# Fused attention and feed-forward on one core: product 2 of seven accumulates onto a copied product 1, more seven-product units, one explicit order for all work

## The chip, the cores and the metric

The kernel runs on one core of a Trainium2 chip. The metric is the device time of one execution in microseconds (us). A core has TensorE (matmuls, "PE", with weight loads as "PEld"), VectorE ("DVE"), ScalarE ("ACT"), GpSimd ("POOL") and SyncE ("SP"); POOL, SP and ACT also issue DMAs. Matmuls write PSUM, which has eight banks of 512 f32 a partition.

## What is computed

Squared-relu attention without a softmax, and on its output a feed-forward block with a gated unit:

```python
scores = (1/sqrt(64)) * q @ k.T          # batch 8, 12 heads, sequence 448, head 64
attn = maximum(scores, 0)**2 / 448
x = (attn @ v) -> (3584, 768)            # heads side by side
g, val = x @ w_gate, x @ w_val           # (768, 1536) each
out = (gelu(g) * val) @ w_out            # (1536, 768)
```

Inputs and output are f32; the kernel computes in bf16 with f32 sums in PSUM.

## The kernel before, in words

**The array.** All large matmuls use a quarter of the array (64 rows by 64 columns, `mm`, line 364, recorded at line 365). The upper and lower row halves are two streams, PE0 and PE1 in the code; each step of a stream is two matmuls, one for each column half.

**The stages.** For each batch, `add_scores` (line 677) makes 21 score units (a relu on ACT, L714, then a square on DVE, L728). `add_values` (line 761) makes six pairs of heads of x, transposed as xT, which are copied from PSUM (L792). `add_gate_value` (line 1023) makes one block of 128 columns of gate or of value with six steps of 448 columns; the gate ends in a gelu (L1044), the value in a multiply (L1049) that writes uT. The last stage, `add_product` (line 1160), makes the output in 14 groups (a to n), each with seven products instead of eight (384 columns wide, copied or added at L1225 and L1223).

**Seven-product units.** Part of gate and value is done in the same manner: `add_pair` (line 911) takes two blocks of gate and of value of a batch as a two by two product, split into halves of the depth and of the tokens, with seven products of six steps of 224 columns. `NPB` (line 317) says how many such units each batch has: 0, 1, 2, 3, 4, 4, 6, 6, in all 26. They need sums of weights (`add_pair_sums`, line 845, four DVE adds) and sums of tokens (`add_token_sums`, line 887). Products 1, 6, 5 and 3 go one after another through one PSUM bank (X), 7 and 4 through a second (Y), 2 has a third (Z). Products 1, 6 and 7 are copied to SBUF by ACT (L962, the tile `part`); 2, 4 and 5 are added to these copies by DVE (L966); then ACT takes the gelu (L970) and DVE multiplies (L975).

**The order.** Nothing is ordered by hand at the level of instructions. Each step becomes an `Op` with a cost, an engine and what it depends on; `run_plan` (line 109) then walks through time and writes the program engine by engine. A later piece of TensorE work is a `Unit`; `next_unit` takes from the next 40 (`AHEAD`) of a list the first that can start at once, together with the bank that came free first. The list is sorted by a place, `at`. For gate, value, units and products the place comes from the string `LINE`: a digit is the next gate or value block of that batch, `3B6` is product 6 of unit B of batch 3, `d7` is product 7 of output group d. Scores and values have places worked out from those of the blocks, moved by the numbers in `SHIFT`. Batch 0's attention follows a list of its own, `START`.

**Banks.** Two banks at first, later one pair, hold scores; six (`FB + 2`) serve all the rest. A Z bank is taken when product 2 starts.

**Loads.** POOL issues the loads of q, k and v and of all weights in one order; from batch 2 on they wait for relus of earlier thirds of a batch (a third is four heads). From batch 2 on q and k are regrouped by DVE (L475) and transposed by DMAs that SP issues (L480), between the stores of the output (L1241).

## Time and profile before

| what | us |
|---|---|
| three timed runs, median | 403.09 |
| three timed runs, lowest and highest | 400.13, 404.37 |
| span of the profiled execution | 394.9 |

The profiled execution has its span, from the first to the last instruction, and no time of its own beside it; the timed runs hold also what lies around the span.

The profile shows one execution. Each group of instructions has a line number, an engine, what it writes and reads, its shape and a count; then its busy time, the mean of one in ns, and the idle time of its engine just before it with what ended that. "PE" is busy from the start to a modelled end of a matmul, and matmuls overlap, so how fast the array runs is read from the distance between starts.

### The profile page before, as it was taken

Reading aid. Unit: us, or ns where it says so; the run is one execution under the profiler, and the core shown is the slowest. Engines: PE = TensorE matmul, PEld = TensorE weight load, DVE = VectorE, ACT = ScalarE, POOL = GpSimd, SP = SyncE. Lnnn points to the kernel's source line nnn. Section 1 sums busy time; section 2 is a strip of 40 time slices with the busy share of each in tenths; the row PEclk is TensorE's granted clock in tenths of the full one; section 3 lists DMA queues with packets and bytes.
Section 4 is the critical chain, followed back from the end, with each engine's and each line's share of the span. In section 5 each row is a group of like instructions: output and inputs, shape, how many; then the busy total and the mean of one; then the engine's idle time right before and its main releaser. Section 6 shows DMA issues by size and latency. Waiting matters only on the chain.

```text
span 394.9 us, 22904 instructions
## 1 busy us (share of the span) xinstructions
PE 386.3 (98%) x10570; PEld 358.4 (91%) x10573; DVE 309.6 (78%) x522; ACT 258.7 (66%) x401; POOL 97.2 (25%) x156
## 2 busy tenths in 40 slices
PE   7999999999999999999999999999999999999995
PEld 3458889999999999999999999989999999999994
DVE  3885779968797499999797779758988999866772
ACT  5866872357677767787786478765787886535541
POOL 7656523322233323232332123310211000000000
PEclk9999999999999999999999999999999999999999
DMA  8999999988999969887999598880763501121134
GB/s 110 186 199 199 197 209 185 112 103 83 161 148 175 152 85 143 93 132 121 113 148 108 124 122 111 139 83 11 103 105 56 125 6 43 45 45 45 43 85 120
DMA packets 85567, 45.12 MB, mean 114 GB/s; under 512 B 46048, under 2 KB 82400, under 8 KB 85472
## 3 DMA queue, kind: packets, MB, share of 16 engines
q0 software_dynamic: 46944, 24.39, 49.9%
q1 hardware_dynamic: 37888, 18.49, 26.4%
q8 instruction: 82, 1.34, 1.4%
q10 hardware_dynamic: 640, 0.79, 0.6%
q14 instruction: 13, 0.11, 0.1%
HBM read 48.76 MB, written 11.01 MB: 151 GB/s over the span
## 4 chain that ended last, share of the span: by engine, by line
PE 93%; DVE 2%; DMA 2%; POOL 1%; issue 1%; ACT 0%; ACTq 0%; POOLq 0%
PE ff L365 85%; PE sp L365 7%; DMA qk<-in_k_dram 2%; DVE attnT L728 1%; PE sp L646 1%; POOL qk L424 1%; DVE xT L792 0%; PE ff L646 0%; ACTq L1241 0%; ACT osb L1225 0%; ACT rl L714 0%; PE ff L567 0%; DVE osb L1223 0%; DVE qkT L650 0%; POOL ident masks.py:199 0%
## 5 line engine op out<-in xcount | busy, mean ns | idle before, releaser
L714 ACT ACTIVATE rl<-sp 128x896 bf16<-128x896 f32 x168 | 152.1, 919 | 50.4 <-PE sp L365 45.1
L365 PE MATMUL ff<-xT,wg 64*64 64x224 bf16 (+1 forms) x2304 | 183.7, 299 | 0.6 <-issue 0.6
L365 PEld LDWEIGHTS <-wv 64*64 64x64 bf16 x2304 | 127.7, 107 | 4.4
L365 PEld LDWEIGHTS <-wg 64*64 64x64 bf16 x2304 | 123.3, 107 | 5.0 <-issue 0.5
L365 PE MATMUL ff<-xT,wv 64*64 64x448 bf16 x1056 | 120.8, 349 | 0.0
L728 DVE TENSOR_TENSOR attnT<-rl 128x1792 bf16<-128x1792 bf16 (+1 forms) x98 | 92.2, 952 | 6.6 <-ACT rl L714 6.2
L365 PEld LDWEIGHTS <-ws 64*64 64x64 bf16 x1872 | 92.3, 107 | 1.4 <-issue 1.0
L365 PEld LDWEIGHTS <-s 64*64 64x64 bf16 x1344 | 81.6, 107 | 1.8
L365 PE MATMUL ff<-attnT,v 64*64 64x448 bf16 (+1 forms) x768 | 79.7, 326 | 0.7 <-DVE attnT L728 0.6
L365 PE MATMUL ff<-ts,wv 64*64 64x224 bf16 x1248 | 78.7, 256 | 0.0
L365 PE MATMUL ff<-ts,ws 64*64 64x224 bf16 x1248 | 77.6, 256 | 0.0
L365 PE MATMUL sp<-qkT 64*64 64x448 bf16 (+1 forms) x768 | 74.6, 328 | 0.7 <-issue 0.3
L365 PE MATMUL ff<-wo,s 64*64 64x384 bf16 x672 | 63.4, 323 | 0.0
L966 DVE TENSOR_TENSOR part<-ff,part 128x448 f32<-128x448 f32 x78 | 47.5, 622 | 20.1 <-PE ff L365 16.4
L365 PEld LDWEIGHTS <-uT 64*64 64x64 bf16 x1008 | 62.5, 107 | 0.7
L365 PE MATMUL ff<-wt,s 64*64 64x384 bf16 x672 | 61.4, 322 | 0.0
L365 PE MATMUL ff<-wo,uT 64*64 64x384 bf16 x672 | 60.7, 322 | 0.0
L962 ACT COPY part<-ff 128x448 f32<-128x448 f32 x78 | 41.3, 534 | 12.4 <-PE ff L365 11.2
L443 POOL DMA_DIRECT2D v<-in_v_dram x48 | 29.6, 620 | 80.3 <-ACT rl L714 44.3
L365 PEld LDWEIGHTS <-v 64*64 64x64 bf16 x768 | 44.7, 107 | 4.1 <-issue 1.7
L424 POOL DMA_DIRECT2D qk<-in_q_dram x43 | 27.6, 642 | 80.0 <-ACT rl L714 59.5
L1049 DVE TENSOR_TENSOR uT<-gel,ff 128x448 bf16<-128x448 bf16 x44 | 27.3, 620 | 22.4 <-PE ff L365 11.0
(51 smaller groups left out, 423.9 us busy)
## 6 DMA issues: line engine op xcount, KB each, us to landing
out_dram<-osb SPq DMA_DIRECT2D x48, 192.0 KB, 3.3
v<-in_v_dram POOLq DMA_DIRECT2D x48, 128.0 KB, 4.1
wg<-in_moe_w_gate_dram POOLq DMA_DIRECT2D x6, 384.0 KB, 10.4
wv<-in_moe_w_val_dram POOLq DMA_DIRECT2D x6, 384.0 KB, 11.0
wo<-in_moe_w_out_dram POOLq DMA_DIRECT2D x4, 576.0 KB, 14.9
qk<-in_q_dram POOLq DMA_DIRECT2D x18, 128.0 KB, 3.5
qk<-in_k_dram POOLq DMA_DIRECT2D x18, 128.0 KB, 4.3
qk<-in_q_dram POOLq DMA_DIRECT2D x18, 96.0 KB, 3.8
```

Source lines behind the costliest of these rows:

```text
L365: ins = nc.tensor.matmul(o, lhsT, rhs, start=start, stop=stop, skip_group_check=onto, tile_position=(P * row, P * col))
L424: return nc.gpsimd.dma_start(qk16[b, m][HALF[i], r0:r0 + h1 - h0, cols], src[b, h0:h1].rearrange("h (p c) d -> p h (c d)", c=SC)[:, :, cols])
L443: return nc.gpsimd.dma_start(v16[b, m][HALF[i], h0 % 4:h0 % 4 + h1 - h0, :, :], v[b, h0:h1].rearrange("h (p c) d -> p h c d", c=SC)[:, :, ...
L646: blocks.add(nc.tensor.transpose(t[HALF[j], c, :], src[:, 2 * r + j, c, :], ident[:, :], tile_position=(0, P * j)))
L714: relu.ins = nc.scalar.activation(duo["rl"][:, u % 2, :, :], box[0][:, :, 0:S], AF.Relu).ins
L728: nc.vector.tensor_tensor(a[:, part], duo["rl"][:, part], duo["rl"][:, part], op=ALU.mult)
L962: rd.ins = nc.scalar.copy(st["t", name][:, :], box[0][:, 0:S]).ins
L966: rd.ins = nc.vector.tensor_tensor(t[:, :], box[0][:, 0:S], t[:, :], op=ALU.add).ins
L1049: u_op[b, fc].ins = nc.vector.tensor_tensor(uT[b][:, fc, :], gel.pop((b, fc))[:, :], box[0][:, 0:S], op=ALU.mult).ins
```

## The change

- **Product 2.** At product 1 the unit now takes two banks, X and Z (`more` in `Unit` and `next_unit`). ACT copies product 1 from X into Z (`emit_seed`), and product 2 accumulates onto it there, so it waits for that copy. The gelu reads Z. The DVE add of product 2 and the SBUF copy of product 1 are gone.
- **Covers.** `full` notes whether a bank's last work had written all its columns. Where it had not (output products, 384 columns), two matmuls of zeros over the remaining columns come first.
- **Banks in the planner.** Work that opens a bank, and isn't the first of its kind in the list, is held back unless `SPARE` (2) banks remain beside those it needs.
- **xT copies.** From batch 1 on such a copy is offered to DVE and to ACT and goes to the first that is free. Before, the second offer stood at the end of a list of which the planner looks at the first 48; now it looks at all.
- **Units.** `NPB` becomes 0, 2, 4, 4, 4, 4, 6, 6, in all 30. (The words that came with the change say 28; `NPB` and `LINE` both hold 30.)
- **The order.** `LINE` now also places scores (`s`), values (`v`), transposes (`t`) and the weight sums (`w3` for pair 3); `SHIFT` and the places worked out from it are gone.

```diff
@@ -10,19 +10,23 @@
...
 LINE = """
-0 0 0 0 0 0 0 0 0 0 0 0 0 0 0 0 0 0 0 0 0 0 0 0 1 1A1 1 2 1A6 2 2 1 1A7 1A2 1A5 2 a1 2 a2 2A1 1A4 1
-1 1 1A3 1 2 1 2A2 a6 1 2A7 a7 2 1 a5 1 1 2A6 2 2 1 1 1 1 a3 1 1 a4 1 1 b1 b7 c1 b2 b6 2A4 2 c6 b4 b5
...
-7F4 7D6 7D5 7D4 7D3 l2 7F5 7A4 7C5 7C3 7E3 7A3 l5 l4 7F3 m1 n1 m7 k3 l3 m2 m6 n6 m5 n7 n4 m3 n5 n2
-m4 n3
+s s s s s s s t s s 0 0 0 s 0 0 0 s s s s t 0 0 s s s s s v 0 v s 0 0 0 0 0 0 v v s s s s 0 0 0 0 0
+v v 0 1 1 a7 1 s 1 w2 0 s s s s s s 1 1A1 1 1 1A2 a1 s 1B1 a6 1 1 w3 w1 s s s w0 1A6 s 1A7 a4 1B7
...
+c1 b7 c7 c6 s b1 b6 b4 b5 2A1 c4 s s s s v 2 2 2 b2 b3 2A6 2A7 2 2B1 2B6 c5 2B7 v v 2B2 2B4 2 2A2
...
+k6 k4 7C1 7C6 7F7 7F5 7F4 7F3 7D4 7B1 7C2 7B2 7C7 7C5 7E1 k5 7B6 7B7 7E7 l5 7B5 7B4 7B3 7D5 7D3 7C4
+7A3 7E6 7E5 7C3 7E2 7E4 m1 m7 7E3 m2 n1 n2 l2 l3 k3 m6 n6 n7 m5 n4 m3 n5 n3 m4
...
@@ -30,9 +34,6 @@
 t00 s0 s1 t01 s2 s3 s4 s5 t10 s6 s7 v0 s8 t11 v1 s9 s10 s11 t20 s12 s13 v2 s14 t21 s15 v3 s16 s17
 s18 s19 v4 s20
 """
-
-
-SHIFT = "-183 -79.5 40.75 1.75 -343.75 -112 43.75 -179.5 27.25 -513.5 -447.25 0.25"
 class Op:
@@ -96,17 +97,20 @@
 class Unit:
-    def __init__(self, at, los, his, box=None, closer=None, prev=None):
+    def __init__(self, at, los, his, box=None, closer=None, prev=None, more=None, full=True):
         self.at, self.los, self.his, self.box, self.closer, self.prev = at, los, his, box, closer, prev
+        self.more, self.full = more, full
         self.begun = False
         self.short = False
 AHEAD = 40
 BANK = 0.3
-
-
-def run_plan(queues, pools, units, banks, arrivals, together, fill, blocks, span):
+COVER = 0.06
+SPARE = 2
+
+
+def run_plan(queues, pools, units, banks, full, arrivals, together, fill, blocks, span):
@@ -157,10 +161,16 @@
     def next_unit(short):
         best = None
+        first = True
+        rest = sum(c is None or c.end is not None for c in banks.values())
         now = max(free["PE0"], floor)
         for u in units[:AHEAD]:
             if u.prev is not None and not u.prev.begun or short and not u.short:
                 continue
+            if u.box is not None:
+                if not first and rest < SPARE + 1 + (u.more is not None):
+                    continue
+                first = False
             t = ready(u.los[0])
             if t is None:
                 continue
@@ -184,11 +194,20 @@
                 if k is None:
                     continue
                 t = max(t, end + BANK)
+            k2 = None
+            if u.more is not None:
+                for n, c in banks.items():
+                    x = 0.0 if c is None else c.end
+                    if n != k and n in full and x is not None and (k2 is None or x < end):
+                        k2, end = n, x
+                if k2 is None:
+                    continue
+                t = max(t, end + BANK)
             if short and t > now:
                 continue
             t = max(t, now)
             if best is None or t < best[0]:
-                best = (t, u, k)
+                best = (t, u, k, k2)
                 if t <= now:
                     break
         return best
@@ -215,7 +234,7 @@
                     best = (key, "PE0", found)
         for e, ops in pools.items():
             mine = None
-            for op in ops[:48]:
+            for op in ops:
                 r = ready(op)
                 if r is not None:
                     t = max(r, free[e], floor if e in together else 0.0)
@@ -231,12 +250,20 @@
         forced = False
         (t, _, _), e, op = best
         if isinstance(op, tuple):
-            _, u, k = op
+            _, u, k, k2 = op
             u.begun = True
             units.remove(u)
             if k is not None:
                 u.box["k"] = k
                 banks[k] = u.closer()
+                full[k] = u.full
+            if k2 is not None:
+                u.more[0]["k"] = k2
+                banks[k2] = u.more[1]()
+                if not full[k2]:
+                    u.more[0]["cover"] = True
+                    u.los[0].cost += COVER
+                full[k2] = True
             queues["PE0"][at["PE0"]:at["PE0"]] = u.los
             pools["PE1"] += u.his
             op = u.los[0]
@@ -314,10 +341,11 @@
     EARLY = 2
     GATE_T, BLOCK = 1.2, 7.1
-    NPB = (0, 1, 2, 3, 4, 4, 6, 6)
+    NPB = (0, 2, 4, 4, 4, 4, 6, 6)
     ROOM = 4
     RING_V, RING_T, RING_H, RING_R, RING_A, RING_O = 3, 3, 2, 2, 4, 4
     SINGLE = "3"
+    RING_L = 2
     RING_M, RING_G = 5, 4
     out_scale = 1.0 / (D * S)
...
@@ -534,7 +562,7 @@
     def next_scores(at):
         n = len(units)
-        if at > WIDE and n % SB == 0 or wide:
+        if n >= WIDE and n % SB == 0 or wide:
             if not wide:
                 wide.append(0)
                 until.update({FB: at, FB + 1: at})
...
@@ -810,6 +838,8 @@
             x_op[b, pr] = Op("DVE", 0.575, emit_copy, [o_op[b, pr]], lag=0.2, prio=1,
                              other=("ACT", 0.5, emit_scaled) if b else None)
             DVE.append(x_op[b, pr])
+            if x_op[b, pr].other is not None:
+                ACT.append(x_op[b, pr])
         bank_read(box["k"], x_op[b, pr])
         if last:
             ops[1][0].after = ops[0][1]
@@ -916,11 +946,15 @@
             add_token_sums(b)
         st = pair_state.setdefault((b, unit), {})
         stage = stages[name]
-        if name in opens:
+        if name in "17":
             st["box", stage] = {}
             free = []
+        elif name == "2":
+            free = [st["read", "1"]]
         else:
             free = [st["read", stage]]
+        if name == "1":
+            st["box", "Z"] = {}
         box = st["box", stage]
         i = blocks[0] * 128 // WCH
         a = {"1": lambda: wg[i][:, KTOP, :], "2": lambda: wg[i][:, KEND, :], "3": lambda: ws[4, i],
@@ -937,6 +971,12 @@
         def emit(r, k):
             if 0 not in box:
                 box[0] = new_bank(box["k"], st["read", stages_last[stage]])
+            if (r, k, name) == (0, 0, "1"):
+                z = st["box", "Z"]
+                z[0] = new_bank(z["k"], st["read", "2"])
+                if "cover" in z:
+                    for j in range(2):
+                        mm(z[0][HALF[j], OGS:], warm[HALF[0], HALF[j]], warm[HALF[0], 0:512 - OGS], 0, j, False, False, True)
             if r == 1 and k == 0:
                 wait_lower(box)
             mov = ts[b, x][:, :, :] if isinstance(x, int) else xT[x[0]][:, x[1], x[2]]
@@ -945,7 +985,7 @@
             for j in range(2):
                 ins = mm(box[0][HALF[j], f * HS:(f + 1) * HS],
                          a()[HALF[r], c, o + P * j:o + P * (j + 1)], mov[HALF[r], c, :], r, j,
-                         name in opens and r == 0 and k == 0, r == 1 and c == K3 - 1, True)
+                         name in "17" and r == 0 and k == 0, r == 1 and c == K3 - 1, True)
             box[1] = ins
         ops = [[Op(f"PE{r}", HW, lambda r=r, k=k: emit(r, k),
@@ -956,6 +996,9 @@
             ts_used[b, x].append(last)
         else:
             reads_x.setdefault(x[0], []).append(last)
+
+        def emit_seed():
+            rd.ins = nc.scalar.copy(st["box", "Z"][0][:, 0:S], box[0][:, 0:S]).ins
         def emit_copy():
             st["t", name] = mpool.tile([128, S], f32, name="part", tag="part")
@@ -997,17 +1040,17 @@
                 u_op[to, f] = m
             return m
-        if name in "167":
+        if name == "1":
+            rd = Op("ACT", 0.5, emit_seed, [last], lag=0.2, prio=0)
+            ACT.append(rd)
+        elif name in "67":
             rd = Op("ACT", 0.5, emit_copy, [last], lag=0.2, prio=0)
             rd.takes = part_ring, lambda: st.get(("end", name))
             ACT.append(rd)
-        elif name in "245":
-            of = {"2": "1", "4": "6", "5": "7"}[name]
+        elif name in "45":
+            of = {"4": "6", "5": "7"}[name]
             rd = Op("DVE", 0.58, lambda: emit_add(of), [last, st["read", of]], lag=0.2, prio=0)
             DVE.append(rd)
-            if name == "2":
-                g = gelu(lambda: st["t", "1"][:, :], [rd], 0.2)
-                st["end", "1"] = g
             st["sum", name] = rd
         else:
             rd = gelu(lambda: box[0][:, 0:S], [last], 0.06)
@@ -1017,7 +1060,8 @@
             st["half"] = mult("2", "6", b0, c0, rd)
         if name == "3":
             mult("3", "7", b1, c1, st["sum", "5"], st["half"])
-        then(at, GS, *ops, box if name in opens else None, lambda: st["read", stages_last[stage]])
+        then(at, GS, *ops, box if name in "17" else None, lambda: st["read", stages_last[stage]],
+             (st["box", "Z"], lambda: st["read", "2"]) if name == "1" else None)
     def add_gate_value(at, b, fc, g):
...
@@ -1301,81 +1345,44 @@
...
+    flow = [[("g", b, fc, g) for fc in range(2 * NPB[b], FC) for g in range(2)] for b in range(B)]
+    flow_s = [(b, u) for b in range(1, B) for u in range(NU)]
+    flow_v = [(b, pr) for b in range(1, B) for pr in range(NPAIR)]
+    flow_t = [(1, m, (0, 1)) for m in range(1, NM)]
     work = []
-    flow = [[("g", b, fc, g) for fc in range(2 * NPB[b], FC) for g in range(2)] for b in range(B)]
-    line = []
...
+    for x in START.split():
+        at = placed0[x.rstrip("a")]
+        n = int(x.rstrip("a")[1:])
+        if x[0] == "t":
+            work.append((at, add_transposes, (0, n // 10, (n % 10,))))
+        else:
+            work.append((at, {"s": add_scores, "v": add_values}[x[0]], (0, n)))
+    work.append((PLACE5, add_values, (0, NPAIR - 1)))
+    work.append((PLACE5 + 0.05, add_transposes, (1, 0, (0, 1))))
+    for g in range(2):
+        work.append((0.0, add_gate_value, flow[0].pop(0)[1:]))
+    for n, x in enumerate(LINE.split()):
+        at = 1.0 + n
+        if x[0] == "w":
+            work.append((0.0, lambda at, i: add_pair_sums(i), (int(x[1]),)))
+        elif x == "s":
+            work.append((at, add_scores, flow_s.pop(0)))
+        elif x == "v":
+            work.append((at, add_values, flow_v.pop(0)))
+        elif x == "t":
+            work.append((at, add_transposes, flow_t.pop(0)))
+        elif len(x) == 1:
+            work.append((at, add_gate_value, flow[int(x)].pop(0)[1:]))
         elif len(x) == 3:
-            line.append(("7", int(x[0]), "ABCDEFGHIJKL".index(x[1]), x[2]))
+            work.append((at, add_pair, (int(x[0]), "ABCDEFGHIJKL".index(x[1]), x[2])))
         else:
-            line.append(("p", "abcdefghijklmn".index(x[0]), x[1]))
-    assert not any(flow)
-    at = 0.0
-    starts = [None] * B
-    placed = []
-    for item in line:
-        if item[0] == "g" and starts[item[1]] is None:
-            starts[item[1]] = at
-        if item[0] == "7" and starts[item[1]] is None:
-            starts[item[1]] = at
-        placed.append((at, item))
-        at += {"g": G, "7": G / 2, "p": R}[item[0]]
-    starts.append(at)
-    WIDE = 20.0
-    for at, item in placed:
-        if item[0] == "g":
-            work.append((at, 5, add_gate_value, item[1:]))
-        elif item[0] == "7":
-            work.append((at, 5, add_pair, item[1:]))
-        else:
-            _, gr, name = item
-            work.append((at, 5, add_product, (gr, name, gr == B * SC // 4 - 1)))
-    LEAD = 6.0
...
-    LO1 = 2.0
-    for b in range(B):
-        if b == 0:
-            lo, hi = -60.0, -12.0
-        elif b == 1:
-            lo, hi = LO1, starts[1] - LEAD
...
-        if b >= EARLY:
-            lo, hi = lo + float(SHIFT.split()[2 * (b - 2)]), hi + float(SHIFT.split()[2 * (b - 2) + 1])
-        if b >= EARLY:
-            lo = max(lo, passed)
-            hi = max(hi, lo + 1.0)
-        passed = hi
-        step = (hi - lo) / NU
...
-            work.append((x, 2, add_values, (b, pr)))
-        for u in range(NU):
-            work.append((placed0[f"s{u}"] if b == 0 else lo + u * step, 3, add_scores, (b, u)))
-    work.sort(key=lambda w: w[:2])
-    for i in reversed(range(max(NPB))):
-        behind = [n for n, w in enumerate(work) if w[2] is add_gate_value and w[3][0] == first_use(i) - 1][-1]
-        work.insert(behind + 1, (0.0, 5, lambda at, i: add_pair_sums(i), (i,)))
-
-
-    for at, _, fn, args in work:
+            gr = "abcdefghijklmn".index(x[0])
+            work.append((at, add_product, (gr, x[1], gr == B * SC // 4 - 1)))
+    assert not any(flow) and not flow_s and not flow_v and not flow_t
+    WIDE = 44
+
+
+    for at, fn, args in work:
         fn(at, *args)
@@ -1457,13 +1464,13 @@
     for made in (x_op, x_first):
         for (b, pr), op in made.items():
             op.deps += reads_x.get(b - 2, ())
-    for op in [*ACT, *DVE]:
-        if op.other is not None:
-            (DVE if op.engine == "ACT" else ACT).append(op)
-
     banks = {k: readers.get(k, [None])[-1] for k in range(FB + 2)}
+    full = {}
     run_plan({"PE0": PE0, "POOL": POOL}, {"PE1": PE1, "ACT": ACT, "DVE": DVE, "SP": SP, "IDLE": IDLE}, later,
-             banks, arrivals, ("PE0", "PE1"), fill, blocks, BLOCK)
+             banks, full, arrivals, ("PE0", "PE1"), fill, blocks, BLOCK)
+    if not rest:
+        for pool in loaded:
+            pool.__exit__(None, None, None)
 # ---- launch: one core; inputs and outputs as the reference has them ----
```

51 lines of the change are left out of this document (17 added, 34 removed).

## The prediction, on record before the change was run

> **What bounds the kernel now.** I read the page first (busy shares and the chain that ended last), then the busy time by stretches, then the groups of matmuls by shape, then what TensorE waited for.
>
> ```profile
> PE 386.3 (98%) x10570; PEld 358.4 (91%) x10573; DVE 309.6 (78%) x522; ACT 258.7 (66%) x401; POOL 97.2 (25%) x156
> ...
> PE 93%; DVE 2%; DMA 2%; POOL 1%; issue 1%; ACT 0%; ACTq 0%; POOLq 0%
> ```
>
> TensorE is busy nearly all the time and is 93% of the chain. A busy TensorE need not run at full rate, so the next question is how far apart its matmuls start. Three timelines give that, one for each width of the moving operand (first column: start in us).
>
> ```profile
> 78.48 0.38 PE L365 MATMUL ff<-xT,wv 64*64 64x448 bf16 x2
> ...
> 79.05 0.38 PE L365 MATMUL ff<-xT,wv 64*64 64x448 bf16 x2
> ```
>
> ```profile
> 264.44 0.26 PE L365 MATMUL ff<-ts,wv 64*64 64x224 bf16 x2
> ...
> 265.01 0.26 PE L365 MATMUL ff<-xT,ws 64*64 64x224 bf16 x2
> ```
>
> ```profile
> 387.49 0.32 PE L365 MATMUL ff<-wt,uT 64*64 64x384 bf16 x1
> ...
> 388.13 0.32 PE L365 MATMUL ff<-wt,uT 64*64 64x384 bf16 x1
> ```
>
> On one row half of the array two matmuls (its two column halves) start together. Three steps of 448 columns take 0.57 us, six of 224 take 0.57, four of 384 take 0.64: a step is 0.190, 0.095 and 0.160 us, and four matmuls (two row halves) share it. Now the groups by shape, with their counts:
>
> ```profile
> L365 PE MATMUL ff<-xT,wv 64*64 64x448 bf16 x1056 | 120.8, 349 | 0.0
> L365 PE MATMUL ff<-xT,wg 64*64 64x448 bf16 x1056 | 119.3, 349 | 0.0
> L365 PE MATMUL ff<-ts,wv 64*64 64x224 bf16 x1248 | 78.7, 256 | 0.0
> L365 PE MATMUL ff<-ts,ws 64*64 64x224 bf16 x1248 | 77.6, 256 | 0.0
> L365 PE MATMUL ff<-xT,wg 64*64 64x224 bf16 x1248 | 76.0, 256 | 0.6 <-issue 0.6
> L365 PE MATMUL ff<-attnT,v 64*64 64x448 bf16 x576 | 72.7, 349 | 0.7 <-DVE attnT L728 0.6
> L365 PE MATMUL sp<-qkT 64*64 64x448 bf16 x576 | 64.7, 351 | 0.4 <-ACT qkT L617 0.2
> L365 PE MATMUL ff<-wo,s 64*64 64x384 bf16 x672 | 63.4, 323 | 0.0
> L365 PE MATMUL ff<-wt,s 64*64 64x384 bf16 x672 | 61.4, 322 | 0.0
> L365 PE MATMUL ff<-wo,uT 64*64 64x384 bf16 x672 | 60.7, 322 | 0.0
> L365 PE MATMUL ff<-xT,ws 64*64 64x224 bf16 x624 | 39.6, 256 | 0.0
> L365 PE MATMUL ff<-wt,uT 64*64 64x384 bf16 x336 | 34.1, 323 | 0.0
> L365 PE MATMUL ff<-attnT,v 64*64 64x224 bf16 x192 | 26.6, 257 | 0.1
> L365 PE MATMUL sp<-qkT 64*64 64x224 bf16 x192 | 11.0, 257 | 0.3 <-issue 0.3
> ```
>
> 448 columns: 3264 matmuls, 816 steps of 0.190 = 155 us. 224 columns: 4752, 1188 steps of 0.095 = 113 us. 384 columns: 2352, 588 steps of 0.160 = 94 us. Together 362 of the 394.9 us of the span: the array streams at full rate for 92% of the time, and only 33 us are not that. Where these lie, by stretches (us, then busy time of PE, PEld, DVE, ACT, POOL):
>
> ```profile
> 0.00:26.00 26.00, 22.25 (x298) 11.48 (x305) 17.18 (x33) 19.70 (x24) 17.74 (x32) 1.00 1.16 160
> 26.00:57.00 31.00, 30.94 (x664) 25.36 (x658) 21.13 (x29) 20.67 (x28) 14.80 (x22) 1.00 1.37 201
> 57.00:250.00 193.00, 193.00 (x5166) 184.65 (x5162) 160.01 (x266) 131.24 (x200) 55.49 (x89) 1.00 0.94 128
> 250.00:270.00 20.00, 19.35 (x640) 18.63 (x634) 13.40 (x24) 13.48 (x24) 3.06 (x5) 1.00 0.72 92
> 270.00:385.00 115.00, 115.00 (x3718) 113.52 (x3713) 95.68 (x171) 72.42 (x125) 6.12 (x10) 1.00 0.32 61
> ```
>
> The first 26 us hold batch 0's attention, about 8 us of streaming (an eighth of the attention groups above: 288 steps of 0.190 and 96 of 0.095), so some 18 are lost there. From 57 to 385 there is nothing to win but work itself: the granted clock is 1.00, TensorE has no idle time but 0.65 us between 250 and 270 (the 0.6 "issue" of the 224-column xT,wg group above). DVE (160.0 of 193) and ACT (131.2) have room. So the change must pay in TensorE's steps, or in the small gaps.
>
> **The change, part by part.**
>
> *Units.* The words that came with the change say 28, but the new table of units per batch, (0, 2, 4, 4, 4, 4, 6, 6), and the units named in the new order both make 30, against 26; I go by these. A unit replaces two blocks of gate and value, 4 groups of 6 steps of 448 columns (24 x 0.190 = 4.56 us), by seven products of 6 steps of 224 (42 x 0.095 = 3.99). It saves 0.57 us; four more save **2.3 us**. With an error of 0.01 us on each of the two intervals the saving per unit could be 0.4 to 0.75, so 1.6 to 3.0.
>
> *Product 2 on a copied product 1.* Vector and scalar work by these rows:
>
> ```profile
> L966 DVE TENSOR_TENSOR part<-ff,part 128x448 f32<-128x448 f32 x78 | 47.5, 622 | 20.1 <-PE ff L365 16.4 <-ACT part L962 3.1
> ...
> L962 ACT COPY part<-ff 128x448 f32<-128x448 f32 x78 | 41.3, 534 | 12.4 <-PE ff L365 11.2 <-DVE uT L975 0.3
> ...
> L792 DVE TENSOR_SCALAR xT<-ff 128x448 bf16<-128x448 f32 x48 | 29.8, 622 | 7.1 <-PE ff L365 6.7
> ```
>
> DVE loses one add per unit (26 x 0.622 = 16.2 us). Each of the four added units brings it two adds, and its two multiplies stand for two of the same size that go: 4 x 2 x 0.622 = +5.0. DVE ends 11 us lower. ACT keeps its copy of product 1 (now into a PSUM bank) and its gelu of the sum (now read from PSUM), and gains 3 copies for each added unit: 4 x 3 x 0.534 = 6.4 us more. All of it lies beside TensorE, which is at full rate while DVE is at 83% and ACT at 68% (57 to 250 us): **0 on the path**.
>
> What the part adds is a wait: product 2 may not start until product 1 has ended and been copied. A turn of that kind can be priced:
>
> ```profile
> 15.46 0.93 ACT rl L714
> ...
> 16.43 0.38 PE sp L365 x4
> ```
>
> ACT starts at 15.46 and takes 0.93, TensorE follows at 16.43, 0.04 us after its end. With 0.53 for the copy and the 0.26 that a matmul of 224 columns is in flight, the turn is 0.53 + 0.26 + 0.04 = 0.83 us. TensorE works strictly in its written order, so everything behind product 2 would wait too. The cover is the other work that the order puts between: in the listed order 25 of 30 units have over 0.6 us of streaming between their 1 and their 2, five have less. But the list is not the program: a planner goes down it with a window of 40 and takes what is ready. Bounds: 0, and 30 x 0.83 = 25 us with no cover at all. I take 0.2, near the lower end, since today's waits of the same sort (an output product behind the read of its bank) cost TensorE nothing from 57 to 385 us.
>
> *Bank covers.* Where the third bank last held an output product (384 columns wide), two matmuls of zeros over the other 128 columns come first, on one row half: 128/224 x 0.095 = 0.054 us, 0 to 30 of them, 0 to 1.6 us. I take a dozen, half hidden behind the other row half: **+0.3**. The same third bank is held longer, from the first matmul of product 1 on: that is a rival below.
>
> *xT copies on either engine.* All 48 copies of the row above ran on DVE; 42 may now move, 0.622 us off DVE for about the 0.53 of an ACT copy. DVE and ACT stand beside TensorE: 0.
>
> *The order.* Scores, values and transposes of batches 1 to 7 get places of their own. A moved score unit takes its relu (ACT), its square (DVE), its loads (POOL issues them behind relus) and its DMA transposes (SP, between the stores) with it:
>
> ```profile
> L475 DVE COPY qkr<-qk x18: 617/620/799, 69.9 to 293.3; 128x1792 bf16<-128x1792 bf16 x18
> ```
>
> The new list asks for batch 2's scores after some 38 us of streaming, sooner than now; but the regrouped q and k of batch 2 exist only from 69.9 us, behind all weights on POOL's queue, whose order is unchanged. The cover is batch 1's gate and value work (16 groups of 1.14 us and two units of 3.99: 26 us), so I put 0 on that. Early, 26 to 57 us hold (counts of that stretch by the same steps) about 29 us of work: 1.7 are lost, of which I take back **-0.5** (bounds -1.7 and, as much the other way, +1.7). Two more pairs of weight sums fall before batch 2 (8 adds of DVE, some 5 us at the 0.62 of the rows above) while DVE gives up some adds and copies: 0. The gap between 250 and 270 us and the thinner steps around it (by counts, 1.2 us) belong to the old order; I take back **-0.8** (bounds -1.2 and 0). At the end the last read is a DVE add where it was an ACT copy, 0.09 dearer by the rows of the products' adds and copies above (0.622 and 0.534, for slightly more columns): **+0.1**.
>
> **Sum**: -2.3 + 0.2 + 0.3 - 0.5 - 0.8 + 0.1 = **-3.0 us**, made against the span of 394.9 us. The three timed runs have a median of 403.09 us (400.13 to 404.37), 8.2 above that span; I take this distance as unchanged: 403.1 - 3.0 = **400.1 us**.
>
> One rule of the Trainium skill speaks against the change. "TensorE: Matmul & The Clock Gate", section "Back-to-back issue gap", says that in a stream of weight loads and matmuls the spacing is about 81 ns at 128 columns and 131 ns at 512. Worked out from it (an estimate, on a straight line): 94 ns at 224 and 123 ns at 448, a unit of 42 x 0.094 = 3.93 us for 24 x 0.123 = 2.94, so four more units would cost 4 us and the sum would be +3.3, 406.4 us. The trace has 0.190 us at 448 columns in its own stream and disagrees, so this gets a chance of 0.01; it would lie within 1%.
>
> **The rivals.**
>
> *Faster by over 1%.* The shorter chain behind product 2 and a lighter DVE close all the small gaps: -2.3 - 1.7 (26 to 57 us) - 1.2 (250 to 270) = -5.2, 397.9 us.
>
> For it: an order that sets every item has more freedom, and the median lies 3 us above the fastest run, so stalls that the profile does not show exist. Against it: the first 26 us keep their own list, and the gaps come from causes not seen.
>
> *Slower: bank waits at product 2.* A unit now holds two banks from its start and a third from product 7; six banks serve all. Where the third comes late, or product 2 stands too near product 1, TensorE waits up to 0.83 us with all its order behind it. Three such waits eat the 2.3 us; at over eight (with 2.3 gone, 8 x 0.83 = 6.6) the change is 4 us, 1%, slower. With ten: -2.3 + 8.3 = +6.0, 409.1 us. For it: the listed order asks for more than six banks at many places, and five units have their 1 and 2 almost side by side. Against it: the planner counts banks and keeps spare ones, and it has met the same kind of limit today at 193.0 busy of 193.
>
> *It does not do what it says*: the steps are saved and lost again in the new order, within 1% either way.
>
> **How the numbers follow.** A measurement of this kernel tells about 1% (4 us) from no change. Forecast, with the lost-again case (within 1% around 400.1, own range 398 to 404): 0.48. Faster rival at 397.9: 0.37. Bank waits: 0.15. Faster by over 1% 0.37, within 1% 0.48, slower 0.15. The range leaves out most of the bank case and little below the faster one (397.9 less a rounding of the units' saving, 0.7, and as much again from stalls not seen): 395.5 to 407.
>
> **What would show it.** TensorE: 384 matmuls of 448 columns on xT fewer (1728, not 2112), 672 of 224 columns more in the units (5040, not 4368), no idle time worth 1 us from 57 us on, the span near 392. DVE near 298 us or, with copies moved, less; ACT over 264. Part adds 60, copies to part 60, 30 copies from PSUM to PSUM near 0.53 us. Wrong would be: waits of TensorE on ACT's copy or on a bank's reader over 2 us in total; the steps of 0.190 and 0.095 changed; loads or transposes of batch 2 ending a wait; a gap of the "issue" kind at more than one place.

## The result, and the profile after

| | median, us | lowest to highest | runs |
|---|---|---|---|
| before | 401.61 | 399.97 to 404.37 | 4 |
| changed | 413.13 | 411.46 to 414.65 | 4 |

The ratio is 1.029 (95% interval 1.023 to 1.035): the change made the kernel slower by 11.5 us, and the time lies above the range (the runs of before are the three shown ahead and one more). The profiled execution of the changed kernel took 412.83 us with a span of 410.9, 16.0 above the span of 394.9 shown before.

The page of the changed kernel, its busy shares, the queue that carries instructions, and the chain that ended last:

```profile
PE 392.2 (95%) x10865; PEld 353.1 (86%) x10865; DVE 288.5 (70%) x479; ACT 277.5 (68%) x438; POOL 96.4 (23%) x156
...
q8 instruction: 85, 1.39, 1.4%
...
PE 92%; issue 3%; DVE 2%; DMA 1%; POOL 1%; ACT 0%; ACTq 0%; POOLq 0%
```

TensorE's busy share fell from 98% to 95%, and "issue" rose from 1% to 3% of the chain: time in which TensorE waited for nothing that the profile shows. Queue q8 carries instructions; its packets are 16 KiB (1.39 MB in 85). Before it had:

```profile
q8 instruction: 82, 1.34, 1.4%
```

That is 10,865 weight loads and 10,865 matmuls over 85 packets: 256 instructions, or 128 matmuls, in a packet. What TensorE waited for between 57 and 310 us, and from there to 395, in the changed kernel (us in total, how often, the longest):

```profile
PE ff L393 <- issue: 9.8, 11, 2.5
```

```profile
PE ff L393 <- issue: 1.2, 3, 0.4
```

No wait for ACT's copy, for a bank's reader or for a DMA stands beside these. Before, all of 57 to 385 us had one such wait:

```profile
PE ff L365 <- issue: 0.6, 1, 0.6
```

Where the largest stand, by the chain of the changed kernel (start, length, what):

```profile
133.50 0.29 PE ff L393 x10
133.79 1.47 issue
135.25 1.31 PE ff L393 x37
136.56 0.03 PE sp L393
136.59 0.00 PE ff L393
136.59 0.16 PE sp L393 x6
136.75 1.65 PE ff L393 x42
138.40 0.18 PE sp L393 x4
138.59 0.67 PE ff L393 x15
139.25 2.47 issue
```

and in its tail, where the pattern can be counted:

```profile
374.33 3.44 PE ff L393 x126
377.78 0.30 issue
378.08 3.31 PE ff L393 x128
381.38 0.44 issue
381.82 3.40 PE ff L393 x126
385.23 0.07 issue
385.29 3.31 PE ff L393 x128
388.60 0.44 issue
389.04 15.05 PE ff L393 x357
```

In the tail TensorE does 128 matmuls, pauses, does 128 more (the chain counts 126 in two of the pieces; by the matmuls' starts it is 128 in each of the four). The other gaps fit the same grid. A gap is a distance of over 0.25 us between the starts of two matmuls. Counted from the first matmul, those of over 0.5 us come after number 82 to 91 modulo 128. The number creeps down because TensorE's queue also holds semaphore instructions, 19 of them between 92 and 332 us; with these counted, 18 of the 19 gaps from 57 us on stand at instruction 192 or 193 modulo 256 (the 19th, 0.28 us at 143.2, lies where the clock is slow, see below). So TensorE stops at the ends of instruction blocks. The trace's DMA records of q8 say why. Each row here is one block of 256 instructions of the changed kernel, in us; the fetch is that of the block behind it:

```
begins  last matmul (after)  fetch starts (after)  takes  ends    next block starts (after it)  gap
blocks beside loads and transposes
130.15  133.53 (3.38)        132.74 (2.59)         1.27   134.01  135.25 (1.25)                 1.72
135.25  138.91 (3.65)        139.18 (3.92)         0.95   140.12  141.72 (1.60)                 2.82
141.72  147.35 (5.62)        142.79 (1.07)         1.19   143.98  147.41 (3.43)                 0.06
155.41  159.16 (3.75)        157.59 (2.18)         0.95   158.53  159.96 (1.43)                 0.80
in the tail, only matmuls of 224 columns
378.08  381.13 (3.05)        379.25 (1.17)         1.29   380.54  381.82 (1.28)                 0.69
385.29  388.34 (3.05)        386.36 (1.07)         1.17   387.54  389.04 (1.50)                 0.69
```

A fetch starts about when the block before has ended or later, takes 0.95 to 1.29 us in these rows, and where TensorE has to wait it goes on 1.2 to 1.6 us after the fetch's end; in none of the profiles of this document did a block begin sooner than 1.20 us after it, from 57 us on. Where delay, fetch and this time together are longer than the work of the block that is running, TensorE stands still. A block of 224-column matmuls holds 128/4 x 0.095 = 3.04 us of work; its fetch in a quiet stretch needs about 1.1 + 1.2 + 1.35 = 3.65. One of 448 columns holds 6.1 us. Before, the same sum was met with little to spare: between 120 and 200 us its 17 blocks held 4.63 us each by the counts of their widths, four of them under 4.2; after the change 4.17 each, ten of 17 under 4.2.

The fetches came later too. In that stretch they started 1.80 us after a block's end on the mean (1.58 in a second profile of the changed kernel; before 1.12, and 1.46 in a second profile of it; both second profiles stand among the experiments), and 1.9 to 3.9 us after it at the seven gaps that stand at block ends. These gaps sum to 8.4 us. An estimate from their lengths: blocks longer by the lost 0.46 us would have saved 3.1 of that, and the rest falls to the later fetches. From 200 us on the blocks hold what they held (4.21 us to 310, before 4.20; 3.80 from there, before 3.74). The 6.9 us of gaps there (before 0.9, second profile 2.3) go with where the new order puts transposes and narrow products, and not with less work in the mean block.

Both kernels reckon with these blocks: `Blocks(256, 256 - 192 + 10, 36, (110, 4))` counts two instructions for a matmul and sets a mark 36 instructions ahead of a block's end, and the planner ties each DMA transpose of SP to such a mark and lets it start only if, by its reckoning, it is done 7.1 us (`BLOCK`) behind the mark. The account of the kernel ahead of the prediction leaves this out. With blocks of 4.2 us, and of 4.6 before, the next end comes before these 7.1 us are over.

The account of the 16.0 us, by the gaps from 57 us on: 16.9 us of them after (1.3 before 120 us, 8.7 from 120 to 200, 4.3 from 200 to 310, 2.6 in the tail), 1.2 before: +15.7. The saved steps give -2.3. Some 1.7 us come from the clock, which fell after the longest gap (busy time by stretches; the eighth column is the granted clock):

```profile
141.70:142.20 0.50, 0.48 (x16) 0.48 (x19) 0.00 (x0) 0.00 (x0) 0.00 (x0) 1.00 1.56 142
142.20:143.20 1.00, 1.00 (x30) 0.99 (x24) 0.58 (x2) 0.00 (x0) 0.00 (x0) 0.59 0.67 85
143.20:144.20 1.00, 1.00 (x24) 0.89 (x19) 1.00 (x3) 0.37 (x1) 0.00 (x0) 0.50 0.00 0
144.20:145.20 1.00, 1.00 (x23) 1.00 (x19) 1.00 (x3) 0.55 (x1) 0.16 (x1) 0.50 0.00 0
145.20:146.20 1.00, 1.00 (x26) 0.98 (x22) 0.64 (x1) 0.09 (x1) 0.45 (x1) 0.70 0.00 0
146.20:147.20 1.00, 1.00 (x42) 1.00 (x38) 0.00 (x0) 1.00 (x2) 0.00 (x0) 1.00 0.84 83
```

0.41 + 0.50 + 0.50 + 0.30 us of streaming lost in four rows. TensorE is "busy" in all of them: the busy column does not show a slow clock, the count of matmuls and the clock column do. Together 15.7 - 2.3 + 1.7 = 15.1 of 16.0; 0.9 us are not placed.

### The profile page after: what moved, and what is told of

Its sections match the earlier page's. It is cut to its first block, busy times and chain, and to the rows that moved or that the text cites. A ratio compares the mean times of both kernels' runs of the same rounds, so it can differ in the third digit from the quotient of the medians.

```text
span 410.9 us, 23522 instructions
## 1 busy us (share of the span) xinstructions
PE 392.2 (95%) x10865; PEld 353.1 (86%) x10865; DVE 288.5 (70%) x479; ACT 277.5 (68%) x438; POOL 96.4 (23%) x156
## 3 DMA queue, kind: packets, MB, share of 16 engines
q8 instruction: 85, 1.39, 1.4%
## 4 chain that ended last, share of the span: by engine, by line
PE 92%; issue 3%; DVE 2%; DMA 1%; POOL 1%; ACT 0%; ACTq 0%; POOLq 0%
PE ff L393 82%; PE sp L393 8%; DVE attnT L756 1%; DMA qk<-in_k_dram 1%; PE sp L674 1%; PE ff L595 1%; PE ff L674 1%; DVE xT L820 0%; POOL qk L452 0%; ACTq L1285 0%; ACT osb L1269 0%; ACT rl L742 0%; DVE osb L1267 0%; DVE qkT L678 0%; POOL ident masks.py:199 0%
## 5 line engine op out<-in xcount | busy, mean ns | idle before, releaser
L393 PEld LDWEIGHTS <-wv 64*64 64x64 bf16 x2304 | 119.5, 107 | 10.4 <-issue 5.5
L393 PEld LDWEIGHTS <-ws 64*64 64x64 bf16 x2160 | 103.5, 107 | 5.0 <-issue 3.9
L393 PE MATMUL ff<-xT,wv 64*64 64x448 bf16 x864 | 97.8, 349 | 0.6 <-issue 0.5
L393 PE MATMUL ff<-ts,wv 64*64 64x224 bf16 x1440 | 91.8, 258 | 3.5 <-issue 3.4
L393 PE MATMUL ff<-ts,ws 64*64 64x224 bf16 x1440 | 92.7, 257 | 0.0
L393 PEld LDWEIGHTS <-uT 64*64 64x64 bf16 x1008 | 59.2, 107 | 2.9 <-issue 1.3
L393 PE MATMUL ff<-wo,s 64*64 64x384 bf16 x672 | 59.7, 323 | 0.0
L1009 DVE TENSOR_TENSOR part<-ff,part 128x448 f32<-128x448 f32 x60 | 36.5, 622 | 28.4 <-PE ff L393 22.7
L393 PE MATMUL ff<-xT,ws 64*64 64x224 bf16 x720 | 46.4, 256 | 1.9 <-issue 1.9
L1013 ACT ACTIVATE gel<-ff 128x448 bf16<-128x448 f32 x60 | 32.6, 546 | 19.3 <-PE ff L393 17.4
```

Of the source, the lines that this page charges most:

```text
L393: ins = nc.tensor.matmul(o, lhsT, rhs, start=start, stop=stop, skip_group_check=onto, tile_position=(P * row, P * col))
L1009: rd.ins = nc.vector.tensor_tensor(t[:, :], box[0][:, 0:S], t[:, :], op=ALU.add).ins
L1013: return nc.scalar.activation(g[:, :], src(), AF.Gelu).ins
```

## The experiments

Theory S (supply): TensorE waits at block ends for its own instructions; the change made blocks shorter in work (more 224-column products, and earlier), and loads and DMA transposes delay the fetches. Rival B: the added wait of product 2 on the copy, or its banks. Rival O: the new order as such. Times are medians; "before" is the kernel before, timed beside that run.

**No DMA transposes from batch 3 on (changed kernel, order kept).** The scores of these batches read the q and k of batch 2.

```diff
     def qkT_tile(b, m):
+        b = min(b, EARLY)
...
         def emit_transpose(i, c0, c1):
+            if b > EARLY:
+                return
```

> The changed kernel, its order on every engine kept, without the 30 DMA transposes of batches 3 to 7 (their scores read batch 2's q and k; loads and regrouping stay). Theory S, instruction supply: TensorE's instructions come in blocks of 256 by a DMA queue of their own; the fetch of a block starts late when transposes and loads hold the DMA engines, and the block is needed before it is there. Then most of the 13 us of TensorE's unexplained gaps from 130 to 300 us go: under 4 us are left there, the 1.3 us gap near 81 us and the five small ones from 371 to 390 us stay, and the span falls from 410.9 to about 400 to 403. Rival B, waits for banks or for the copy of product 1: transposes have no part in those, so the gaps stay and the span stays within 2 us of 410.9.

406.70 us, before 401.61, ratio 1.015 (1.008 to 1.021). Its waits in 57 to 412 us:

```profile
PE ff L393 <- issue: 6.2, 10, 1.3
PE ff L393 <- ACT gel L1016: 0.7, 1, 0.7
```

The gaps from 120 to 310 us fell from 13.0 to 2.9 us, as theory S said, and the mean delay of a fetch from 120 to 200 us from 1.80 to 1.26. The span of 404.9 is longer than the 400 to 403 expected: the gaps before 120 us, where batch 2's transposes remain, rose from 1.3 to 3.2 us, and those of the tail, where there never were any, from 2.6 to 5.1. Why they rose stays open.

**Nor loads and regrouping copies of q and k from batch 3 on.**

```diff
         def emit(c0, c1):
+            if b > EARLY:
+                return None
...
         def emit_copy():
+            if b > EARLY:
+                return
```

> As the run without transposes, and the loads of q and k of batches 3 to 7 and their regrouping copies are left out as well (v, the weights and the stores stay). Theory S: with loads gone too, fetches from 130 to 300 us start within about 1 us of the block boundary, gaps there fall under 1.5 us in all, span about 398 to 401. If the transposes alone are to blame it is no faster than the run without transposes, within 1 us. Rival B: no change, 409 to 413.

401.11 us, ratio 1.000 (0.997 to 1.003):

```profile
PE ff L393 <- issue: 2.7, 6, 1.0
```

0.7 us of gaps are left from 120 to 310; the gap at 81 us (batch 2's transposes are still there) remains, and those of the tail sum to 4.0. With the same program on TensorE the traffic of q and k is worth some 12 to 15 us (413.1, and 415.8 at another time, to 401.1).

**Product 2 without its wait.** Product 2 opens its bank afresh, and the copy of product 1 goes to a tile that nobody reads, so the sum lacks product 1.

```diff
-                         name in "17" and r == 0 and k == 0, r == 1 and c == K3 - 1, True)
+                         name in "172" and r == 0 and k == 0, r == 1 and c == K3 - 1, True)
...
-            rd.ins = nc.scalar.copy(st["box", "Z"][0][:, 0:S], box[0][:, 0:S]).ins
+            rd.ins = nc.scalar.copy(spare[:, :], box[0][:, 0:S]).ins
```

> The changed kernel, its order on every engine kept, but product 2 opens its bank afresh and product 1's copy goes to an unused SBUF tile, so that product 2 waits for no copy (product 1 is left out of the sum). Rival B: if the wait for the copy makes the gaps, 5 to 11 us come back, span 400 to 406. Theory S: the copy has no part in it, span within 2 us of 410.9 and the same gaps at the same block boundaries.

416.06 us, ratio 1.038 (1.031 to 1.045), gaps of 17.9 us where the changed kernel had 16.9:

```profile
PE ff L393 <- issue: 10.7, 17, 2.0
PE ff L393 <- PE sp L393: 0.3, 1, 0.3
```

Rival B falls as far as the copy goes: without the wait nothing is won. The banks are held as before here; against them speaks that no wait for a bank's reader is listed, and that the run before this one closed most gaps with the banks untouched.

**The tail's narrow products mixed with wider ones.** In the list, the output products j to l (384 columns) are spread evenly among batch 7's units:

```diff
-j4 s 6C5 v 6C3 k7 k2 6E4 7A2 6E3 7A6 7A7 6F3 l7 j5 j3 7A5 l1 l6 7D1 7F1 7D7 7F2 7F6 7A4 7D2 7D6 l4
+j4 s 6C5 v 6C3 k7 k2 6E4 7A2 6E3 7A6 7A7 6F3 l7 7A5 7D1 7F1 7D7 j5 7F2 7F6 7A4 7D2 j3 7D6 7C1 7C6 l1
...
```

> The changed kernel with the output products j to l of the last part of the listed order spread evenly between the 224-column products of batch 7, not in clumps; all before 330 us as it was. Theory S: the five gaps from 371 to 390 us (2.6 us) stand where whole blocks hold 224-column products alone: 128 matmuls are 32 steps of 0.095, 3.0 us, and a fetch cycle there takes 3.4 to 3.75 us. With 384-column products in each block the gaps go, span 2 to 3 us less, 408 to 409. Rival B: the gaps follow the products and banks, no change beyond 0.5 us.

417.84 us, ratio 1.041 (1.035 to 1.048). The tail's gaps went from 2.6 to 0.8 us as theory S said, but the time did not follow: the gaps from 57 to 310 us, where the program is the same, summed to 18.1 us instead of 14.3. And from 310 to 385 us some 2.8 us more were lost without a gap; the last experiment shows how. The longer gaps asked for a control.

**The changed kernel again, unaltered.**

> The changed kernel itself, unaltered, on another chip or load, to learn how far the same program's gaps move. Theory S (TensorE waits for its own instruction blocks): the gaps stand at the same block boundaries (one every 256 instructions, 128 matmuls), most of them the same ones, their sum within 10 to 22 us; time 409 to 418. Rival (a chance event of one execution, nothing in the program): gaps at other matmuls, or gone, time near 400.

415.80 us, before 402.65, ratio 1.033 (1.027 to 1.039):

```profile
PE ff L393 <- issue: 13.0, 15, 3.0
```

Gaps of 3.0, 7.9, 5.0 and 2.9 us in the four stretches; 16 of its 19 gaps stand at the same blocks as in the first profile. The gaps belong to the program; the shared ones differ in length by up to 0.8 us, and one of 1.4 us is new, so single gaps and differences of 2 us between runs taken at different times say little.

**More instructions late in the kernel before.**

```diff
+        if len(padded) >= 8400 and len(padded) % 4 == 0:
+            nc.tensor.reg_mov(n_reg, 0)
```

> The kernel before, with one extra register move on TensorE's queue after every fourth matmul from matmul 8400 (about 310 us) on: 543 small instructions, no work taken or added for the array, nothing moved. A block of 256 instructions then holds 114 matmuls instead of 128, about 3.3 us of streaming instead of 3.7, below the 3.4 to 3.75 us that a block took in the changed kernel's tail. Theory S: new gaps at block boundaries from 310 us on, 3 to 9 us in all, about 6, ratio 1.008 to 1.022. Rival (issue is not short, the register moves hide behind streaming as the weight loads do): no gaps, ratio within 0.5% of 1. Rival (each move costs the queue time itself): time lost evenly between the matmuls and not at the boundaries.

402.12 us, ratio 1.001 (0.997 to 1.005). This tells nothing of the theory: the moves are not in the program that ran.

```profile
PE 389.2 (98%) x10570; PEld 358.5 (90%) x10573; DVE 309.7 (78%) x522; ACT 258.5 (65%) x401; POOL 97.1 (24%) x156
...
q8 instruction: 82, 1.34, 1.5%
```

82 packets, as without them, and block ends still 128 matmuls apart. It is of use as a second profiled execution of the kernel before: its span is 398.2 against 394.9, with 4.4 us of gaps, where the one shown had 1.2. Of the other runs of before that were timed beside the experiments none has a span under 395.8 us, and the middle one is near 399, so the profile on which the prediction rests was a lucky execution.

**A shorter time allowed to a transpose behind its mark (changed kernel).** The marks are those of `Blocks`, ahead of a block's end.

```diff
-    GATE_T, BLOCK = 1.2, 7.1
+    GATE_T, BLOCK = 1.2, 5.5
```

> The changed kernel with the span that the planner allows a DMA transpose after its mark cut from 7.1 to 5.5 us, so that a transpose is less often under way when the next instruction block is to be fetched. The planner lets the order of TensorE differ from about matmul 1480 on; the work is the same. Theory S: the fetches start sooner after a boundary (mean delay between 120 and 200 us below the 1.65 of the changed kernel) and the gaps between 57 and 310 us sum to less than 14 us, ratio to before 1.005 to 1.025; the five gaps of the tail stay. Rival (the gaps come from TensorE's new order alone, transposes have no part): the sum stays within 2 us of the changed kernel's in this call.

414.57 us, ratio 1.034 (1.025 to 1.043), beside 415.80 for the control. The gaps from 57 to 310 us fell to 9.0 us (control 15.9), while the mean delay of a fetch from 120 to 200 us hardly moved (1.59; control 1.58). The time did not follow: the planner made another order of it, and from 57 to 310 us that order lost some 4 us more than the control without a gap. Inconclusive.

**xT copies on either engine, alone, on the kernel before.**

```diff
-            for op in ops[:48]:
+            for op in ops[:200]:
```

> The kernel before with the one edit that copies of xT of batch 1 to 7 are really offered to either engine (the planner looks at 200 waiting operations of an engine, not 48). The prediction put 0 on it. Theory S: TensorE's order shifts a little with it, the count and mix of its instructions do not; time within 1% of before, DVE a few us less busy, ACT a few more, and any gap over 0.25 us stands at a block boundary. Rival (the copies on ACT delay relus or gelus, and this is what slows the changed kernel): waits of TensorE on ACT of over 2 us, ratio above 1.01.

407.77 us, ratio 1.014 (1.008 to 1.020): outside what theory S allowed. The waits it names are 2.1 us of "issue", none on ACT, so the copies themselves delay nothing:

```profile
PE ff L365 <- issue: 2.1, 4, 0.9
```

With this edit the planner wrote another order from matmul 600 on, and several of its gaps are not at block ends. Much of the loss has no gap at all: from 325 to 375 us matmuls started that stream for 43.5 us in 50 (by the median steps of the trace, 0.189, 0.163 and 0.096 us), with TensorE busy throughout, where before had 49.9. So a new order can cost several us in a way of its own; the last experiment shows what that looks like.

**Shorter blocks in the kernel before.** The direct test: half of the 448-column steps of plain gate and value blocks, from matmul 2470 to 4670, are cut into two of 224. The planner does not count the added matmuls.

```diff
+            cut = 2470 <= len(splits) <= 4670 and dc in (1, 2, 3)
+            for h in range(2 if cut else 1):
+                for j in range(2):
+                    cs = slice(h * S // 2, (h + 1) * S // 2) if cut else slice(0, S)
...
```

> The kernel before; between its matmuls 2470 and 4670 (some 120 to 200 us) half of the 448-column steps of the plain gate and value blocks are each cut into two of 224 columns. The same columns stream in the same order, no wait is added; TensorE only has some 280 matmuls and as many weight loads more. A block of 128 matmuls in that stretch then holds about 4.1 us of streaming, not 4.6 (the changed kernel has 4.2 there). Theory S (blocks too short for their fetch): new gaps at block boundaries in that stretch, 3 to 10 us in all (the changed kernel had 8.4 there), ratio 1.008 to 1.025, and none elsewhere that before does not have. Rival (the changed kernel's loss comes from its order, banks or waits, not from the number of instructions): no new gap, ratio within 0.7% of 1.

409.64 us, before 401.81, ratio 1.021 (1.016 to 1.025). TensorE's waits from 120 to 200 us, and its chain at the largest:

```profile
PE ff L365 <- issue: 4.8, 5, 2.7
```

```profile
153.61 0.38 PE ff L365 x16
153.99 2.69 issue
156.68 2.45 PE ff L365 x22
```

The fetch behind the block that began at 149.94 started 4.16 us later, the block held 3.80 us, and the next began 1.36 us after the fetch's end: the picture of the changed kernel. Gaps from 120 to 200 us sum to 7.2 us (kernel before: 0.0 and 0.7 in its two profiles; changed: 8.7). Blocks held 4.13 us, the changed kernel's 4.17. No order, no wait and no column was changed, only the number of instructions, and most of the loss of that stretch came back. Rivals B and O do not do that. It does not part shorter blocks from later fetches, though: since the planner's count leaves the added matmuls out, the marks of the transposes no longer stand ahead of the real block ends, and fetches started 1.85 us after a block's end (before 1.12, padded run 1.46). The transpose issued at 149.1 us stood 0.80 us ahead of its block's end and landed 7.5 us later, after the late fetch; in the kernel before, the same one stands 3.62 us ahead of an end. Gaps of 2.0 us from 200 to 310 us and of 2.2 after were not expected; the padded run of before had 1.6 and 0.7 there. Whether the displaced marks have a part in them is not shown.

**More transposed bytes in the kernel before.**

```diff
             one[:] = [ins]
+            nc.sync.dma_start_transpose(
+                spare[:, :, :, :].rearrange("d c r x -> d (c r) x"),
+                qkr[b, m][:, c0:c0 + 2].rearrange("p c h d -> p (c h d)"))
```

> The kernel before, with a further DMA transpose of two chunks into a spare tile behind each one of its DMA transposes (four sevenths more transposed bytes); TensorE's program is unaltered. Theory S: fetches of instruction blocks start later (mean delay between 57 and 310 us above the 0.5 to 1.1 us of before), gaps at block boundaries of 2 to 8 us in all, ratio 1.004 to 1.02. Rival (transposes do not touch the fetches): no gaps, ratio within 0.5% of 1. Another rival: scores become late and TensorE waits for qkT.

410.51 us, ratio 1.021 (1.015 to 1.027). Fetches started 1.56, 2.03 and 1.14 us after a block's end in 57 to 120, 120 to 200 and 200 to 310 us (before 1.05, 1.12, 0.66; in the padded run 1.28, 1.46, 0.93), and the gaps there sum to 12.3 us, more than expected, with some 1.5 us of waits for ACT among them, which are not at block ends. TensorE's program was as it was: later fetches are enough to bring gaps at block ends.

**Both kernels without the traffic of q and k.** The edits of the second experiment, on the kernel before, and on the changed kernel with the mixed tail.

> The kernel before without loads of q and k, regrouping copies and DMA transposes from batch 3 on (scores read batch 2's q and k), the order on every engine as it was: the counterpart of the second experiment. Theory S: before has no gaps worth naming in that stretch, so there is little to win: 397 to 401 us, ratio 0.985 to 1.0. Rival (the traffic slows every kernel alike, and its removal says nothing of the change): a gain as large as that of the changed kernel, 9 to 13 us, to about 390.

397.52 us, ratio 0.990 (0.985 to 0.994), and TensorE waits for nothing from 57 us to the end. So the kernel before loses some 4 us in its median run to this traffic, about what the gaps of its second profile sum to (4.4). The changed kernel without the traffic (401.11, the second experiment) lies 3.6 us above: its gaps, most of them in the tail and before 120 us, sum to 6.0 us against 0.3 here, and 2.3 us of steps are saved. So of the 11.5 us some 8 come with the traffic of q and k from batch 3 on, and the rest with gaps that stay without it.

> The changed kernel without that same traffic and with the tail's output products mixed among its narrow products: both places where its blocks outran their fetches are relieved. Theory S: 397 to 400 us, at most one gap of 1 us, and 0 to 3 us below the kernel before without that traffic in this call, as the step counts say (2.3 us of streaming saved). Rival (another cost stays that no gap shows): 402 us or more.

401.41 us, ratio 1.000 (0.998 to 1.004): 3.9 us above its counterpart, where 0 to 3 below was expected. The supply is nearly met (gaps of 2.8 us in all, one wait of 0.6 us in its list), so something else costs. From 350 to 375 us this kernel starts matmuls for 21.9 us of streaming in 25, its counterpart for 24.6, and neither has a gap over 0.3 us there. The timeline of this kernel shows it:

```profile
365.91 0.35 PE L393 MATMUL ff<-wo,s 64*64 64x384 bf16 x2
365.96 0.35 PE L393 MATMUL ff<-ts,wv 64*64 64x224 bf16 x3
366.07 0.32 PE L393 MATMUL ff<-wo,s 64*64 64x384 bf16 x1
366.08 0.26 PE L393 MATMUL ff<-ts,wv 64*64 64x224 bf16 x1
366.10 0.32 PE L393 MATMUL ff<-wo,s 64*64 64x384 bf16 x1
366.23 0.77 PE L393 MATMUL ff<-xT,wg 64*64 64x224 bf16 x12
366.81 0.48 PE L393 MATMUL ff<-ts,wv 64*64 64x224 bf16 x6
```

Up to 366.1 two products run side by side, one on each row half. The twelve matmuls of xT,wg then run alone: 0.58 us from 366.23 to 366.81, six steps of 0.097, where two halves side by side do 24 matmuls in that time. TensorE is fully busy and works at half rate. This lies in the part that was mixed. The changed kernel itself streams for 47.0 us from 350 to 400, and 2.6 of the missing 3.0 are the gaps of its tail; so this loss belongs to the mixing and not to the change. Whether the changed kernel with its supply met would run below 397.5 stays open. No version of the changed kernel that was run beats the kernel before.

## Why the prediction was wrong, point by point

- **The bound.** "From 57 to 385 there is nothing to win but work itself" was read from busy time. That TensorE had a second limit close by was in the traces unread: q8's 82 packets, and the single "issue" gap. It stood in the code as well, in `Blocks`. The step that put the gap between 250 and 270 us down to the order ("belong to the old order; I take back -0.8") misread it. It was a block end: its fetch started at 263.29 us, took 1.35, and the next matmul came at 266.12, 1.5 us after the fetch's end.
- **The step that failed** is "So the change must pay in TensorE's steps, or in the small gaps": the units were priced by steps alone, and the loads and DMA transposes that a moved score unit takes with it were listed and then priced at nothing. A unit saves 0.57 us of streaming and adds 168 - 96 = 72 matmuls with their weight loads: 144 instructions. Four units are 2.25 blocks; the new table of units also moves them forward (batches 1 to 3 had 6 units, now 10), into the stretch of their loads and transposes. In place of -3.0 us the runs show 16.9 us of gaps, nearly all at block ends where TensorE waits for its own instructions, against 1.2: blocks that hold less work up to 200 us, and fetches that come later up to 310. Cutting steps in the kernel before from 120 to 200 us brought 7.2 us of gaps, where the change brought 8.7; taking the traffic of q and k away took all but 0.7 of the 13.0 us from 120 to 310. How the loss divides between shorter blocks and later fetches is only estimated.
- **Units, -2.3.** Right in itself: 1728 and 5040 matmuls came as counted, and the steps are still 0.19 and 0.095 us.

```profile
L393 PE MATMUL ff<-xT,wg 64*64 64x448 bf16 x864 | 98.3, 353 | 2.5 <-issue 2.5
L393 PE MATMUL ff<-xT,wv 64*64 64x448 bf16 x864 | 97.8, 349 | 0.6 <-issue 0.5
...
L393 PE MATMUL ff<-warm 64*64 64x128 bf16 x4 | 0.5, 216 | 0.0
```

- **Covers, +0.3.** Two of thirty units needed one (the four matmuls of the last row): 2 x 0.054 = 0.1 us at most.
- **Product 2's wait, +0.2.** Too dear, if anything: no such wait shows, and without it nothing was won. The copy costs what was put on it (0.525, predicted "near 0.53"):

```profile
L1001 ACT COPY ff<-ff 128x448 f32<-128x448 f32 x30 | 15.7, 525 | 6.8 <-PE ff L393 5.6
...
L832 ACT ACTIVATE xT<-ff 128x448 bf16<-128x448 f32 x25 | 13.6, 544 | 11.3 <-PE ff L393 10.3
```

- **xT copies, 0.** 25 of 48 went to ACT at 0.544 us. DVE's 288.5 and ACT's 277.5 are as the sums say, and TensorE never waited for either in that stretch. Alone on the kernel before, the edit cost 1.4% through the order that followed from it, which the prediction did not price at all.
- **The order, -0.5 and -0.8, and the tail, +0.1.** Neither gain came, and the tail lost 2.6 us in gaps: 640 matmuls of 224 columns stand there without a wider one between, five blocks of 3.04 us each against a fetch of some 3.65.
- **The span and the median.** The 8.2 us between the profile's span and the median were taken as unchanged. In the runs of before a time lies 1.9 to 3.7 us above its span, so at least 4.5 of the 8.2 us are a span longer than the one profiled: that profile was luckier than the median, and the prediction took it for the rule.
- **The rivals.** The one on the slower side had the right sign (409.1 us with ten waits) and the wrong mechanism: no bank decided, and that its figure is the nearest is luck. "A gap of the 'issue' kind at more than one place" had been named as a sign of being wrong, and is what came; but it had no price and no chance.
- **The rule on the spacing of matmuls** was rejected rightly; its 406.4 rested on steps that the trace still does not have. The page that bore on the case was another: the Trainium skill, "Runtime: NRT & Kernel Launch", section "Instruction fetch mechanics", says that instructions come in blocks of 256 over a DMA queue of the engine's own. The trace agrees with 82 and 85 packets of 16 KiB. It also says that the cost of crossing a block is mostly hidden; in this kernel it was, before the change, with little to spare, but the wait of 2.47 us at 139.25 was not hidden.

## What to carry to other kernels

Count TensorE's instructions by stage, not only its columns: here a block of 256 must hold about 3.7 us of streaming in a quiet stretch, or the next one comes too late. Beside loads and transposes the need was 1.8 + 1.1 + 1.3 = 4.2 us on the mean (120 to 200 us, changed kernel) and over 6 for the latest fetch (3.92 + 0.95 + 1.60). An edit that trades wide matmuls for more narrow ones pays in blocks, and one that moves transposes pays where they stand ahead of a block's end. "Issue" waits that stand 128 matmuls apart, or at multiples of that, point to this limit, even when a single one of 0.6 us is all that the profile of before shows.

## What the runs showed of the hardware

- A fetch of 16 KiB of instructions took 0.9 to 2.2 us in the changed kernel, and where TensorE waited for it the first matmul of its block came 1.2 to 1.6 us after its end. Its start moved with other transfers: on the mean 0.4 to 0.9 us after a block's end from 120 us on without the traffic of q and k, 1.8 with it (120 to 200 us, changed kernel), 2.0 with more transposes (before), up to 4.2 (cut steps).
- After TensorE stood still for 2.5 us the granted clock was 0.50 for some 3.4 us; it fell in the same way after waits of 3.0 us in the control and 2.7 in the kernel with cut steps. After a wait of 2.0 us it fell in one run (product 2 without its wait) and stayed 1.00 in another (mixed tail); after the waits of 1.5 us it stayed 1.00. The Trainium skill, "TensorE: Matmul & The Clock Gate", Part 1, gives two states, half and full, and a window of about 3.4 us; both agree with the rows, though the idle time here was shorter than that window.
- A copy from PSUM to PSUM on ACT took 0.525 us, one of the same size from PSUM to SBUF 0.535.
